# A delta-rule attention with a gated feed-forward network: a first pair prepared apart, 48-row transfers, matmuls on zeros and a new order

## The chip, the cores and the metric

The kernel runs on one core of a Trainium2 chip. The metric is the device time of one execution in microseconds (us), less being better. Engines are called as in the profile: PE (TensorE matmul), PEld (its weight load), DVE (VectorE), ACT (ScalarE), POOL (GpSimd) and SP (SyncE, which here only issues transfers). "SPq" and "ACTq" are the issues of transfers on SP and ACT.

## The reference

Four batches of eight heads run a recurrence over 768 steps with a 40 x 40 state each; its outputs go through a small gated network.

```python
for t in range(S):                      # S = 768, D = 40, B = 4, H = 8
    y[:, :, t] = einsum('bhd,bhde->bhe', rt, state)
    Sa = einsum('bhde,bhe->bhd', state, at)
    state = state * wt[:, :, None, :] - einsum('bhd,bhe->bhde', Sa, bt) \
            + einsum('bhd,bhe->bhde', vt, kt)
x = y.transpose(0, 2, 1, 3).reshape(B, S, 320)
h = maximum(x @ w_in, 0)                # w_in is 320 x 1024
conv = sum over k of conv_w[k] * h shifted by k - 1   # 3 taps along S
out = (h * sigmoid(conv)) @ w_out       # w_out is 1024 x 320
```

## The kernel before

The 768 time steps are cut into 24 chunks of 32, called steps n here, and two steps make a pair j (12 pairs). The network works on windows of two steps (12 windows). A pair is prepared with no knowledge of the state; only the "chain" carries the state from one step to the next.

Preparing a pair: `load_wakb` brings w, a, k and b into three rotating tiles in0 to in2. `decays` turns w on PE (tile pw) and makes running products by scans on DVE (suf, pre). `decayed` turns a (pa), writes ah, spreads ah by six transfers into a64, then turns k and b (pk, pb), writes kt and spreads it by six transfers into k64. `spread` cuts each half into three transfers of 40 rows. `scores` multiplies a64 and k64 on PE (ps), and DVE masks the result into "at". `solve_in` sends "at" to DRAM (bd) and back in another layout (bb). `solve` inverts 128 triangular 32 x 32 matrices at once: 31 rounds of a product (st) and a sum (xx), on DVE for five pairs and on POOL for seven, by the letters of SOLVER ("vgggvgvgvgvg"). It ends with xx going to DRAM (xd) and back (tt), all on SP. `hats` turns kt into kb for the chain.

A step of the chain: pp from the state and v, psb on ACT, pu from tt and psb on PE, vu copies on DVE and ACT, pn on PE, the new state on DVE, and its decay (L665) on POOL. `vturn`, `sturn`, `pairs`, `from_state` and `outputs` make the chunk's outputs, `finish` scales them into xh and xl, and `moe_pack` moves some rows of xh and xl by two transfers. `moe_in` and `moe_out` are the network's matmuls (ph and po) with their work on ACT and DVE. The weights arrive as 64-bit floats in 23 pieces (wi, cv, wo, wp). DVE converts each in seven instructions (L278 to L295), and for wi ACT and POOL make the high and the low part (wih, L311, and wil, L313).

Each piece of work is a generator that yields between its parts. ORDER is a list of some 2,000 tokens ("so0*3" is three parts of solve 0), which `emit_all` goes through; so the order within each engine is written out by hand, and an engine works its queue in order. SP issues nearly all transfers in the order of these tokens; for pair 0 alone `queue` sends half of the loads and of the spreading transfers by ACT. POOL and DVE share the two buffers of the tag stmp for st.

Of the kernel before, what the change touches and what calls it, by code (L numbers as in the profile page):

```python
# [8 lines left out]
F32 = mybir.dt.float32  # L9
# [9 lines left out]
C = 32  # L19
# [4 lines left out]
    ld=3, kb=3, pre=3, kt=1, ah64=2, at=3, bb=2, xx=2, stmp=2,  # L24
    tt=2, psb=1, sd=1, vu64=1, ms=1, xf=1, xh=2, xl=2, hb=2, cc=2, o=1,
# [3 lines left out]
    dd="decayed", sc="scores", ha="hats", si="solve_in", so="solve", co="combine",  # L29
    ch="chain", rt="rturn", vt="vturn", st="sturn", pa="pairs",  # L30
    fs="from_state", ou="outputs", fi="finish", pk="pack", mi="moe_in", mo="moe_out", en="end",
# [8 lines left out]
lr1*2 we16 ch1*2 ha3 dd2 vt0 ou0*2 fi0 we18 we14 fi0 ch1 ha3 dd2*2 ch1 so1*2 dd2*2 vt1*2 so1 we18  # L40
so1*2 fs1*2 ld3*2 rt1 ch1 ch2 we17 we0 we15*2 dd2 so1 pa1 rt1 ch2 we20 pa1 ou1 de3 we17 fi0 we21 fi0
ou1 fi1*2 st2*2 fi1*2 pk0 de3 we19 ch2*3 sc4*2 lv3 sc5*2 si2 ha4*2 ch2*3 ro0 fs2 vt2*2 we21 mi0.0*4
ch3 st3*2 we19 ch3*2 dd3*3 mi0.1 we22 si2 ch3*2 mi0.0 fs2 pa2*2 we20 mi0.1*2 mi0.0 vt3*2 ou2*2 ha5
so2 ch3 ha5 ch3 mi0.0 mi0.3 fi2*2 lr2 mi0.2 lr0 fi2 mi0.0 so2*2 ld3*2 dd3 mi0.3*3 dd3 mi0.1*2 dd3
# [977 lines left out]
```

## Time and profile before

| | before |
|---|---|
| median of 3 runs | 639.4 us (637.51 to 640.18) |
| profiled execution | 637.57 us, its span 635.8 us |
| PE | 533.7 us busy (84%) |
| DVE | 450.4 us (71%) |
| ACT, POOL | 268.1 us, 264.3 us (42% each) |
| mean granted clock of PE | 0.911 of full speed |
| DMA | 66.84 MB, 105 GB/s on average |

The page cuts the span into 40 slices and gives the busy tenths of each engine in them. PE's digits begin with 2624267 and are at 7 to 9 from then on, so the first 100 us differ from the rest. DVE begins with 4898899. The chain that ended last is 29% PE, 17% POOL, 16% DVE, 16% DMA and 8% SP's issues. Durations stand in one profiled execution, whose time lies 1.8 us under the median of the runs.

### The profile page before, as it was taken

To read this page: it belongs to the slowest core of one execution; us is meant where nothing else is said; L and a number is where in the kernel's file an instruction comes from. 1 tells how busy PE (TensorE), PEld (TensorE's weight loads), DVE (VectorE), ACT (ScalarE), POOL (GpSimd) and SP (SyncE) were. 2 spreads that over 40 slices of the span, in tenths; PEclk is the share of its full clock that TensorE was granted. 3 is DMA by queue.
4 is the path that set the end of the run, shared out by engine and by line. 5 is a ranking of instruction groups with operands and counts; after the bars stand their busy time and mean duration, and the time that the engine had idled before them with its cause. 6 is when DMAs were issued, how large, how long until landed. Compare 5 with 4: busy or idle time off the path is not lost.

```text
span 635.8 us, 28901 instructions
## 1 busy us (share of the span) xinstructions
PE 533.7 (84%) x12729; PEld 450.9 (71%) x12729; DVE 450.4 (71%) x1030; ACT 268.1 (42%) x568; POOL 264.3 (42%) x532
## 2 busy tenths in 40 slices
PE   2624267798989878899899799899999899999998
PEld 1523256687877767778778698687888678887884
DVE  4898899978775488577687476788677776472661
ACT  4010122445543424445424456324646226563662
POOL 5110368228888201288301585102684104881100
PEclk9555657999999979899999989799999999999999
DMA  8969748568665377476586654564754754211101
GB/s 144 163 116 147 137 93 182 134 113 134 119 115 117 72 122 134 95 123 118 106 138 109 121 114 86 111 119 85 129 113 73 135 109 90 40 30 46 25 10 38
DMA packets 266517, 66.84 MB, mean 105 GB/s; under 512 B 239536, under 2 KB 260936, under 8 KB 266392
## 3 DMA queue, kind: packets, MB, share of 16 engines
q1 hardware_dynamic: 260052, 63.62, 54.8%
q10 hardware_dynamic: 6340, 1.38, 1.2%
q8 instruction: 100, 1.64, 1.1%
q14 instruction: 25, 0.20, 0.1%
HBM read 38.30 MB, written 10.22 MB: 76 GB/s over the span
## 4 chain that ended last, share of the span: by engine, by line
PE 29%; POOL 17%; DVE 16%; DMA 16%; issue 10%; SPq 8%; ACT 4%; POOLq 0%; DVEq 0%; ACTq 0%
POOL xx L580 7%; POOL st L574 7%; PE ph L819 7%; PE po L866 5%; DMA bb<-bd 3%; DMA bd<-at 3%; DMA xd<-xx 3%; DVE cc L848 3%; PE ps L518 2%; DVE xx L580 2%; POOL state L665 2%; DVE st L574 2%; PE pm L720 2%; DMA in<-in_w_dram 2%; SPq L553 2%
## 5 line engine op out<-in xcount | busy, mean ns | idle before, releaser
L848 DVE SCALAR_TENSOR_TENSOR cc<-hb,cw,cc 128x256 f32<-128x256 f32 x192 | 96.5, 562 | 36.2 <-ACT cc L840 36.1
L866 PE MATMUL po<-wo,g 128*128 128x320 f32 x384 | 116.7, 441 | 0.4 <-DVE g L858 0.4
L574 POOL TENSOR_TENSOR st<-xx,bb 128x126 f32<-128x126 f32 (+22 forms) x217 | 88.7, 409 | 39.0 <-DMA bb<-bd 13.9
L580 POOL TENSOR_TENSOR xx<-xx,st 128x126 f32<-128x126 f32 (+22 forms) x217 | 92.0, 424 | 17.0
L665 POOL TENSOR_TENSOR state<-state,a 104x640 f32<-104x640 f32 x23 | 36.6, 1592 | 136.8 <-DVE state L660 108.4
L866 PEld LDWEIGHTS po<-wo,g 128*128 128x128 f32 x384 | 68.3, 190 | 23.2 <-DVE g L858 0.9
L819 PE MATMUL ph<-xh,wih 120*128 120x256 f32 x288 | 72.7, 312 | 0.8 <-issue 0.8
L796 POOL TENSOR_TENSOR xl<-xf,xh 120x384 fp32r<-120x384 f32 x24 | 24.5, 1020 | 95.0 <-ACT xh L794 95.0
L518 PE MATMUL ps<-a,k 104*64 104x64 f32 x768 | 33.1, 246 | 24.0 <-DMA k<-kt 19.6
L819 PEld LDWEIGHTS ph<-xh,wih 120*128 120x128 f32 x288 | 49.0, 194 | 3.7 <-ACT hb L833 0.8
L858 DVE TENSOR_TENSOR g<-cc,hb 128x512 f32<-128x512 f32 x48 | 34.9, 731 | 21.6 <-ACT cc L853 21.3
L574 DVE TENSOR_TENSOR st<-xx,bb 128x56 f32<-128x56 f32 (+22 forms) x155 | 42.3, 273 | 10.4 <-DMA bb<-bd 5.5
L518 PEld LDWEIGHTS ps<-a,k 104*64 104x64 f32 x768 | 29.6, 158 | 28.0 <-issue 21.1
L580 DVE TENSOR_TENSOR xx<-xx,st 128x56 f32<-128x56 f32 (+22 forms) x155 | 41.2, 266 | 5.3
L853 ACT ACTIVATE cc<-cc 128x512 f32<-128x512 f32 x48 | 30.2, 630 | 33.5 <-DVE cc L848 33.4
L694 ACT COPY v<-pv 128x1024 f32<-128x1024 f32 x24 | 24.3, 1013 | 46.4 <-PE pv L674 46.3
L840 ACT ACTIVATE cc<-hb,cw 128x256 f32<-128x256 f32 x96 | 43.5, 501 | 0.1
L833 ACT ACTIVATE hb<-ph 128x512 f32<-128x512 f32 x48 | 28.5, 595 | 33.5 <-PE ph L819 33.5
L636 DVE COPY vu<-pu 32x320 f32<-32x320 f32 x48 | 23.7, 493 | 26.1 <-PE pu L624 25.0
L819 PE MATMUL ph<-xl,wih 120*128 120x256 f32 x192 | 39.3, 287 | 0.0
L819 PE MATMUL ph<-xh,wil 120*128 120x256 f32 x192 | 39.2, 286 | 0.0
L684 ACT COPY r<-pr 64x1024 f32<-64x1024 f32 x24 | 24.1, 1005 | 21.2 <-PE pr L674 16.2
(287 smaller groups left out, 1076.0 us busy)
## 6 DMA issues: line engine op xcount, KB each, us to landing
bb<-bd SPq DMA_DIRECT2D x24, 256.0 KB
k<-kt SPq DMA_DIRECT2D x46, 120.0 KB
a<-ah SPq DMA_DIRECT2D x33, 121.9 KB
rin<-in_r_dram SPq DMA_DIRECT2D x24, 160.0 KB
vu<-in_v_dram SPq DMA_DIRECT2D x96, 40.0 KB
in<-in_w_dram SPq DMA_DIRECT2D x23, 160.0 KB
in<-in_a_dram SPq DMA_DIRECT2D x23, 160.0 KB
in<-in_k_dram SPq DMA_DIRECT2D x23, 160.0 KB
```

What stands on the lines that cost most here:

```text
L518: nc.tensor.matmul(ps[half(z), h * 64 : h * 64 + 64], k64[:SR, NH * c + h, z], pd["a64"][:SR, NH * (2 * z + c) + h, 1:], start=True, stop= ...
L574: eng.tensor_tensor(t3, xx[:, 0:nj, i : i + 1].to_broadcast([128, nj, nt]), bb[:, i : i + 1, i + 1 :].to_broadcast([128, nj, nt]), ALU.mult,)
L580: eng.tensor_tensor(xx[:, 0:nj, i + 1 :], xx[:, 0:nj, i + 1 :], t3, ALU.add)
L665: nc.gpsimd.tensor_tensor(new, new, al.to_broadcast([SR, 2, H, D]), ALU.mult)
L796: nc.gpsimd.tensor_tensor(wd["xl"][:, :, :, tw], xf, xh.bitcast(F32), ALU.subtract)
L819: nc.tensor.matmul(ph[:, j], l[:, fs], x, start=(j == 0 and i == 0), stop=(i == len(passes) - 1), skip_group_check=True,)
L833: nc.scalar.activation(out=hb[:, :, :, 2 : W + 2], in_=ph, func=AF.Relu)
L840: nc.scalar.activation(out=cc[:, j], in_=hb[:, j, :, 1 : W + 1], func=AF.Copy, scale=cw[:, 1, f : f + 1],)
L848: nc.vector.scalar_tensor_tensor(out=cc[:, j], in0=hb[:, j, :, x : W + x], scalar=cw[:, x, f : f + 1], in1=cc[:, j], op0=ALU.mult, op1=ALU ...
L853: nc.scalar.activation(out=cc, in_=cc, func=AF.Sigmoid)
L858: nc.vector.tensor_tensor(g, cc, hb[:, :, :, 1 : W + 1], ALU.mult)
L866: nc.tensor.matmul(po[:rows, :DM], parts(f), wo[:, f, :], start=(f == 0), stop=(f == NF - 1))
```

## The change

- The new function `keys` holds what was the second half of `decayed`: turning k and b, writing kt and spreading it into k64. It has tokens of its own ("ke"). kt becomes one fixed tile with 128 rows.
- For pair 0 the loads come in the order w, k, a, b. For pair 0 the bd, bb and tt transfers alternate between SP and ACT, as the loads did.
- `spread` takes the number of rows: 48 instead of 40 for a64 (both halves) and for the second half of k64; the first half of k64 stays at 40. The extra rows of the sources are cleared once. In `moe_pack` the transfer within xh carries 48 rows, that from xh to xl stays at 40.
- In `decayed` the small copies on ACT (L478, now L481) come before the products on DVE. `decays` has a further yield.
- The clears of a64 and r64 on ACT become a generator ("cl") and stand behind the copies into ah of pair 0.
- `stmp` becomes one buffer for DVE's solves and one, `stg`, for POOL's.
- `warm`: six blocks of four matmuls of a zero matrix with xini, 512 columns each, written to a bank that nobody reads. One stands ahead of the scores (ps) of pair 0, the others ahead of first matmuls ph of windows 0, 3 and 7 and ahead of the transposes of pair 4 (pw) and pair 5 (pk).
- ORDER is drawn anew as a whole.

```diff
-        for x, nm in ((w, "w"), (a, "a"), (k, "k"), (b, "b")):
-            t = ins[(4 * pd["j"] + "wakb".index(nm)) % len(ins)]
+        for i, nm in enumerate("wkab" if pd["j"] == 0 else "wakb"):
+            x = dict(w=w, a=a, k=k, b=b)[nm]
+            t = ins[(4 * pd["j"] + i) % len(ins)]
...
-    def spread(pd, eng, dst, src):
+    def spread(pd, ns, dst, src):
         for y in range(2):
+            n = ns[y]
             for i in range(3):
-                to = dst(half(y, D), y)[:, i::3]
-                queue(pd, y, eng).dma_start(to, src(slice(i * D, i * D + D), y)[:, : to.shape[1]])
+                to = dst(half(y, n), y)[:, i::3]
+                queue(pd, y).dma_start(to, src(slice(i * D, i * D + n), y)[:, : to.shape[1]])
...
         spread(
-            pd, nc.sync, lambda rows, y: k64[rows].rearrange("p n z t -> p n (z t)"),
+            pd, (D, 48), lambda rows, y: k64[rows].rearrange("p n z t -> p n (z t)"),
...
-            nc.sync.dma_start(
+            queue(pd, bi % 2).dma_start(
                 bd[nb * bi : nb * bi + nb].rearrange("n s t -> s n t"),
...
-            nc.sync.dma_start(bb[q * NBL : (q + 1) * NBL], bd)
+            queue(pd, q).dma_start(bb[q * NBL : (q + 1) * NBL], bd)
...
-            tmp = buf(wn, [128, 144], "stmp", f"st{j}_{i}")
+            tmp = buf(wn, [128, 144], "stmp" if SOLVER[j] == "v" else "stg", f"st{j}_{i}")
...
-        nc.sync.dma_start(xh[2 * D : GR, 2].bitcast(F32), xh[0:D, 2].bitcast(F32))
+        nc.sync.dma_start(xh[2 * D : 128, 2].bitcast(F32), xh[0:48, 2].bitcast(F32))
...
+    def warm(i):
+        pz = bank(f"warm{i}")
+        for _ in range(4):
+            nc.tensor.matmul(
+                pz[:, 0:512], zst, xini.rearrange("p j t -> p (j t)"), start=True, stop=True, skip_group_check=True,
+            )
+        yield
...
-we4 we0 ld0*2 de0*2 ld0*2 we3 we2 dd0 ld1 dd0*8 ha1 we0 de1*2 we0 we2*2 we0 we2 we6 we3 we2 sc0 we4
+fs0 we1 ld0*2 de0 ld0*2 we0 we1*3 we2 dd0 de0 dd0 de0 cl0*2 ke0 we4 dd0 ke0*3 dd0 ke0 ha0*2 we4*2
```

What the new ORDER does is seen in the instructions of an engine. In the rows below a number behind a name is the buffer's; wi10q is the piece of w_in that is being converted, xx_437 and xx_440 are the matrices of solve 0, xx_749 and xx_783 those of solve 1.

DVE at the start of solve 0, before: the last instruction of a conversion, kt of pair 1 from b, and the solve.

```order
L295 TENSOR_TENSOR wi10q<-wi10q 120x256
L495 TENSOR_TENSOR kt_375<-pb_399,suf 120x6x64
L495 TENSOR_TENSOR kt_375<-pb_399,suf 120x6x2x32
L567 CAST xx_437<-xini 128x512
L574 TENSOR_TENSOR st_0_439<-xx_437,bb_361 128x31
```

DVE now, at the end of solve 0, where kt of pair 1 stands:

```order
L591 TENSOR_TENSOR xx_440<-xx_440,st_30_555 128x16
L506 TENSOR_TENSOR kt<-pk_485,suf 120x6x2x32
L506 TENSOR_TENSOR kt<-pk_485,suf 120x6x64
L506 TENSOR_TENSOR kt<-pb_567,suf 120x6x64
L506 TENSOR_TENSOR kt<-pb_567,suf 120x6x2x32
L284 TENSOR_SCALAR wi02q<-wi02r 120x256
```

kt of pair 1 has moved from ahead of solve 0 to behind it.

DVE in the middle of solve 0, before:

```order
L574 TENSOR_TENSOR st_11_472<-xx_437,bb_361 128x120
L580 TENSOR_TENSOR xx_437<-xx_437,st_11_472 128x6x20
L278 TENSOR_SCALAR wi22q<-wi22r 80x256
L282 TENSOR_SCALAR wi22q<-wi22r 80x256
L286 SCALAR_TENSOR_TENSOR wi22q<-wi22r,wi22q 80x256
L290 SCALAR_TENSOR_TENSOR wi22q<-wi22q 80x256
L291 TENSOR_SCALAR wi22q<-wi22q 80x256
L292 SCALAR_TENSOR_TENSOR wi22q<-wi22r,wi22q 80x256
L295 TENSOR_TENSOR wi22q<-wi22q 80x256
L574 TENSOR_TENSOR st_12_515<-xx_437,bb_361 128x133
L580 TENSOR_TENSOR xx_437<-xx_437,st_12_515 128x7x19
```

DVE in the middle of solve 0 now:

```order
L585 TENSOR_TENSOR st_10_478<-xx_440,bb_334 128x126
L591 TENSOR_TENSOR xx_440<-xx_440,st_10_478 128x6x21
L585 TENSOR_TENSOR st_11_481<-xx_440,bb_334 128x120
L591 TENSOR_TENSOR xx_440<-xx_440,st_11_481 128x6x20
L585 TENSOR_TENSOR st_12_494<-xx_440,bb_334 128x133
L591 TENSOR_TENSOR xx_440<-xx_440,st_12_494 128x7x19
```

The conversion of wi22 between the rounds 11 and 12 has left the solve (as have that of wi21 and the two masks of pair 1 between the rounds 19 and 20), so that its rounds follow one another from the first to the last.

POOL in the middle of solve 1, before, with four subtractions for wil and the decay of step 0's new state in it:

```order
L580 TENSOR_TENSOR xx_749<-xx_749,st_11_784 128x6x20
L313 TENSOR_TENSOR wil<-wi12q,wih 120x256
L313 TENSOR_TENSOR wil<-wi23q,wih 80x256
L665 TENSOR_TENSOR state_140<-state_140,a_119 104x16x40
L313 TENSOR_TENSOR wil<-wi13q,wih 120x256
L313 TENSOR_TENSOR wil<-wi03q,wih 120x256
L574 TENSOR_TENSOR st_12_1145<-xx_749,bb_558 128x133
```

POOL now, ahead of solve 1:

```order
L319 TENSOR_TENSOR wil<-wi22q,wih 80x256
L676 TENSOR_TENSOR state_140<-state_140,a_119 104x16x40
L319 TENSOR_TENSOR wil<-wi02q,wih 120x256
L578 CAST xx_783<-xini 128x512
L585 TENSOR_TENSOR st_0_785<-xx_783,bb_748 128x31
L591 TENSOR_TENSOR xx_783<-xx_783,st_0_785 128x31
```

The decay of the state stands ahead of solve 1; two subtractions (wi12, wi23) are left within it, behind its eighth round, and the other two stand behind it.

## Rows read from the trace of the kernel before

**Rows 1.** Stages: us, busy PE, PEld, DVE, ACT, POOL; clock, DMA share, GB/s

```profile
0.00:123.00 123.00, 59.79 (x1129) 50.71 (x1129) 103.71 (x258) 27.67 (x46) 48.30 (x107) 0.65 0.76 137
123.00:180.00 57.00, 53.32 (x1211) 47.36 (x1212) 45.84 (x88) 27.76 (x57) 36.18 (x84) 0.97 0.74 129
180.00:375.00 195.00, 173.18 (x4739) 147.02 (x4738) 131.72 (x304) 83.43 (x179) 86.61 (x172) 0.96 0.62 113
375.00:630.00 255.00, 244.46 (x5645) 205.03 (x5645) 169.17 (x383) 128.51 (x287) 93.16 (x172) 0.99 0.42 80
```

**Rows 2.** Waits of PE after 128 us, the k64 transfers: us, times, longest

```profile
PE ps L518 <- DMA k<-kt: 0.5, 2, 0.3
```

**Rows 3.** Timeline, start: start us, us, engine, line, operation, [idle before]

```profile
8.99 0.87 PE L442 MATMUL pw<-ident,in 128*120 128x128 f32 x3 [7.00 <-DMA in<-in_w_dram]
...
18.10 1.02 DVE L495 TENSOR_TENSOR kt<-pb,suf 120x384 f32<-120x384 f32 x2 [1.30 <-PE pb L442]
...
33.84 1.28 DVE L524 TENSOR_TENSOR at<-ps,tris 128x512 f32<-128x512 f32 x2
```

**Rows 4.** Timeline, solve 0 to step 0

```profile
43.69 0.59 DVE L574 TENSOR_TENSOR st<-xx,bb 128x31 f32<-128x31 f32 x1
...
50.69 0.28 DVE L278 TENSOR_SCALAR wi22q<-wi22r 80x256 int32<-80x256 int32 x1
...
53.24 0.28 DVE L574 TENSOR_TENSOR st<-xx,bb 128x133 f32<-128x133 f32 x1
...
73.65 0.40 SPq L583 DMA_DIRECT2D xd<-xx  x1
...
80.09 2.45 PE L624 MATMUL pu<-psb,tt 32*32 32x40 f32 x64 [0.80 <-DMA tt<-xd]
```

**Rows 5.** Timeline, solve 1 to step 4

```profile
74.85 0.24 POOL L574 TENSOR_TENSOR st<-xx,bb 128x31 f32<-128x31 f32 x1 [8.97 <-DVE pre L460]
...
85.76 0.77 POOL L313 TENSOR_TENSOR wil<-wi12q,wih 120x256 fp32r<-120x256 f32 x1
...
94.00 0.42 POOL L574 TENSOR_TENSOR st<-xx,bb 128x133 f32<-128x133 f32 x1
...
112.16 0.39 POOL L580 TENSOR_TENSOR xx<-xx,st 128x16 f32<-128x16 f32 x1
...
115.78 0.46 SPq L583 DMA_DIRECT2D xd<-xx  x1
...
123.72 0.99 PE L624 MATMUL pu<-psb,tt 32*32 32x40 f32 x60 [0.55 <-DMA tt<-xd]
...
139.89 0.24 POOL L574 TENSOR_TENSOR st<-xx,bb 128x31 f32<-128x31 f32 x1 [6.62 <-DMA bb<-bd]
...
182.59 1.08 PE L624 MATMUL pu<-psb,tt 32*32 32x40 f32 x60 [0.26 <-DMA tt<-xd]
```

**Rows 6.** Issues by line on SP: duration ns min/median/max, first and last start

```profile
L426 SPq DMA_DIRECT2D k<-kt x69: 767/768/1615, 18.8 to 518.6; - x69
...
L586 SPq DMA_DIRECT2D tt<-xd x48: 325/413/1463, 77.9 to 573.8; - x48
```

**Rows 7.** Groups up to 128 us: count, busy us, mean ns, idle before

```profile
L574 DVE TENSOR_TENSOR st<-xx,bb 128x126 f32<-128x126 f32 (+22 forms) x31 | 8.7, 281 | 1.0
L580 DVE TENSOR_TENSOR xx<-xx,st 128x126 f32<-128x126 f32 (+22 forms) x31 | 8.6, 277 | 1.1
L460 DVE TENSOR_TENSOR_SCAN pre<-pw,dp 120x396 f32<-120x396 f32 x8 | 7.4, 969 | 0.1
```

**Rows 8.** Timeline, the k64 transfers of pair 1 and its scores

```profile
46.28 5.00 SPq L426 DMA_DIRECT2D k<-kt  x6
...
54.90 0.48 PE L518 MATMUL ps<-a,k 104*64 104x64 f32 x4 [14.66 <-DMA k<-kt]
```

**Rows 9.** Timeline, scores of pair 2 on PE

```profile
124.65 3.49 PE L518 MATMUL ps<-a,k 104*64 104x64 f32 x64
```

**Rows 10.** Chain that ended last: start us, us, what

```profile
378.69 0.95 PE ph L819 x8
```

More of the change, by code (lines that the diff above doesn't have):

```diff
@@ L28 @@
     we="weights", ro="rows", ld="wakb", lv="v", lr="r", de="decays",
-    dd="decayed", sc="scores", ha="hats", si="solve_in", so="solve", co="combine",
+    dd="decayed", ke="keys", sc="scores", ha="hats", si="solve_in", so="solve", co="combine",
     ch="chain", rt="rturn", vt="vturn", st="sturn", pa="pairs",
-    fs="from_state", ou="outputs", fi="finish", pk="pack", mi="moe_in", mo="moe_out", en="end",
+    fs="from_state", ou="outputs", fi="finish", pk="pack", mi="moe_in", mo="moe_out", en="end", wa="warm", cl="clears",
@@ L40 @@
[L40 to L44, printed above, removed]
@@ L241, in tile_decay_delta_attention_then_conv_gate_moe @@
         t = cp.tile([128, 4 * NH, 2 * C + 1], F32, name=f"a64{i}")
-        clear(t.rearrange("p n w -> p (n w)"))
         a64s.append(t)
     ah = [
-        cp.tile([GR, NR, (y + 1) * C + 1], F32, name=f"ah{y}") for y in range(2)
+        cp.tile([128, NR, (y + 1) * C + 1], F32, name=f"ah{y}") for y in range(2)
     ]
     nc.gpsimd.memset(ah[1], 0.0)
+    nc.gpsimd.memset(ah[0][96:128], 0.0)
+    kt = cp.tile([128, 2, 2 * G, 4, C], F32, name="kt")
+    nc.gpsimd.memset(kt[96:128, 1], 0.0)
     k64 = cp.tile([128, 2 * NH - 1, 2, 64], F32, name="k64")
@@ L471, in decayed @@
         for y in range(2):
-            nc.vector.tensor_tensor(
-                ah[y][:, :, C * y + 1 : C * y + C + 1], pa[:, y].rearrange("p (n w) -> p n w", w=C),
-                pd["pre"][:, y, :, 0:C], ALU.mult,
-            )
-        yield
-        for y in range(2):
             nc.scalar.copy(
-                ah[y][:, :, 0], suf[:, y * NY : y * NY + NY].rearrange(
+                ah[y][:GR, :, 0], suf[:, y * NY : y * NY + NY].rearrange(
                     "p (n w) -> p n w", w=C + 1
@@ L483, in decayed, with keys @@
         yield
+        for y in range(2):
+            nc.vector.tensor_tensor(
+                ah[y][:GR, :, C * y + 1 : C * y + C + 1], pa[:, y].rearrange("p (n w) -> p n w", w=C),
+                pd["pre"][:, y, :, 0:C], ALU.mult,
+            )
+        yield
         a64 = pd["a64"] = a64s[j % len(a64s)]
         spread(
-            pd, nc.sync, lambda rows, y: a64[rows, :, 0 : C * y + C + 1], lambda rows, y: ah[y][rows],
+            pd, (48, 48), lambda rows, y: a64[rows, :, 0 : C * y + C + 1], lambda rows, y: ah[y][rows],
         )
         yield
-        kt = pd["kt"] = buf(wn, [GR, 2, 2 * G, 4, C], "kt", f"kt{j}")
+    def keys(pd):
+        j = pd["j"]
         for x, nm in enumerate("kb"):
@@ L585, in solve @@
         for bi in range(B):
-            nc.sync.dma_start(
+            queue(pd, bi % 2).dma_start(
                 tt[quad(bi)].rearrange("p c h t -> p (c h t)"),
@@ L913, in tile_decay_delta_attention_then_conv_gate_moe, with clears @@
     BUFS.update(e1=1, e2=1)
+    def clears():
+        for t in a64s:
+            clear(t.rearrange("p n w -> p (n w)"))
+        yield
+        clear(r64.rearrange("p y i z c x t -> p (y i z c x t)"))
+        yield
+    def warm(i):
[3 more added lines that the diff above has]
+                pz[:, 0:512], zst, xini.rearrange("p j t -> p (j t)"), start=True, stop=True, skip_group_check=True,
+            )
+        yield
     pds = [dict(j=j) for j in range(NSTEP // 2)]
@@ L990, in tile_decay_delta_attention_then_conv_gate_moe @@
     put(("end", 0), moe_end)
+    put(("clears", 0), clears)
+    for i in range(NWARM):
+        put(("warm", i), lambda i=i: warm(i))
     with tc.manual_schedule():
```

180 lines of the change are left out of this document (95 added, 85 removed).

## The prediction

> **What bounds the kernel now.** I read the busy time of the engines by stages first [rows 1]. In the first 123 us PE is busy for 59.8 us, at a mean granted clock of 0.65; from there to 630 us it is busy for 471.0 of 507 us, at 0.96 to 0.99. So there are two regimes: a start in which PE waits for data, and a long stretch in which PE's own work sets the pace, with 3.7, 21.8 and 10.5 us of idle time in its three parts. With two clock levels, 2.4 and 1.2 GHz, means of 0.97, 0.96 and 0.99 make (0.03 x 57 + 0.04 x 195 + 0.01 x 255) / 0.5 = 24 us at the lower one. In the second regime PE waits 0.5 us in all for the k64 transfers [rows 2], so what only makes these transfers quicker is worth nearly nothing there.
>
> Then I followed the start in order of time. The first transposes wait for w's load until 8.99 us, kt of pair 0 is finished at 19.12, and the masked scores "at", for which two rows of DVE are enough, only at 35.12, as DVE converts weights first [rows 3]. Solve 0 starts on DVE at 43.69, is interrupted at 50.69 for a conversion, and its result is sent at 73.65; "pu" of step 0 can begin at 80.09 [rows 4]. Solve 1 runs on POOL from 74.85 to 112.55. Its result is sent at 115.78, and step 2 gets its "tt" at 123.72; solve 2 starts at 139.89, and step 4 has its "tt" at 182.59 [rows 5]. This chain of solves paces the start, and DVE, busy 103.7 of 123 us [rows 1], lies under it.
>
> **First loads and pair 0.** One weight transfer of 240 KB stands ahead of w on SP where two did. At the 137 GB/s of the stage [rows 1] it takes 1.8 us; I take 1.2 of that for kt (0 to 1.8): finished at 17.9. The clears move from ACT's idle beginning behind the copies into ah; only a640 is needed at once, and its transfers wait for the product ah1 anyway. Price nothing; if uncovered, the first two clears' few us on ACT. Between kt and "at" DVE now has three conversions. One is the stretch from 50.69 to 53.24, 2.6 us [rows 4], so DVE is free at 25.7, and PE's scores, moved up with kt, end at about 28.3: "at" is done at 29 instead of 35.1. From "at" to the solve it was 8.6 us [rows 3, 4]; bd and bb now go out on SP and ACT, three issues fewer in a row at 0.41 us (that of tt) [rows 6], plus some queueing, so 7 us: bb is there at 36. On DVE a decays step (four scans of 0.97 us [rows 7] and 0.3), a conversion, two ah products and the cast stand ahead, 8.4 us, so solve 0 starts at about 38. Uninterrupted it has 62 instructions of 17.3 us [rows 7] and gaps: end at 56.5, 14 us earlier than now. xd follows at once; from xd to "pu" it was 6.4 us [rows 4], with tt on two queues 6: step 0 at 62.5 instead of 80.1.
>
> **Why these 17 us don't arrive.** kt of pair 1 now stands behind the whole of solve 0 on DVE; it stood ahead. So kt comes at 58.5, and its six transfers stand behind tt on SP, which waits for xd until 61. Six of 40 rows take 5.0 us to issue, and the first landed 3.6 us after the last was issued, the rest a little later [rows 8]; with three of 48 rows I take 3.7 and 4, so 69.5. Scores at the low clock, up to 3.9 us (3.5 in [rows 9]), "at" at 74, bd and bb on SP alone 8.6: solve 1 starts at about 82.6, not at 74.85. It gets shorter. Now 8.2 us of pause for four subtractions and a state lie in it, from 85.76 to 94.00 [rows 5], then two subtractions (1.6): 31 us, end at 113.6 against 112.55. What saves it is the queue: xd waited 3.2 us on SP behind six k64 transfers and now stands behind two loads of r. Sent at 113.7, with the 7.9 us from 115.78 to 123.72 [rows 5], step 2 gets its tt at 121.6: **2 us** earlier. Bounds: 9 earlier (transfers landing at once, scores at the full clock) to 5 later (below).
>
> **Pair 2.** Its scores stood behind "pu" of step 2 on PE (124.65, 3.5 us [rows 9]); now they stand ahead, in what was idle: **3.5 us**. So bd and bb of pair 2 go out right behind tt, and solve 2 can start once step 2's state has left POOL, at about 130: 10 us earlier. Step 4 follows at about 173, not 182.6.
>
> **48 rows.** Nine of a pair's twelve spreading transfers and one of two in the pack step carry 48 rows. An issue of 40 rows takes 768 ns whatever its bytes, one of 32 rows (tt) 413 [rows 6]; 48 rows lie between these or at the upper, so SP gains 0 to 3.2 us a pair. Beyond the start I book nothing [rows 2]; cover gone, it is SP's to lose.
>
> The Trainium skill, page "DMA: Bandwidth & Descriptors", section "Why a DMA increments its semaphore by 16 and not by 1", says that a transfer runs on the largest number of engines, at most 16, that divides the slowest dimension: 10 engines for 40 rows, 16 for 48. By it each engine carries 3 rows instead of 4; an estimate from that is a quarter off the moving part of the 3.6 us that a transfer took to land, so under 0.9 us for each pair, and the sum would gain that once, ahead of solve 1. The 768 against 413 ns agree with a special case for 40 rows; no row shows the engines themselves.
>
> **Zeros.** Each block is four matmuls over 512 columns. The nearest row is eight of 256 columns in 0.95 us [rows 10], so 0.95 a block at the full clock, twice that at the low one. The first block lies in idle time; five more cost 0 (all in idle) to 4.8 us. I take 2.4.
>
> **POOL and DVE temporaries** now have a buffer each; within one engine the products and sums follow one another anyway, so I book 0.
>
> **The redrawn order.** With PE saturated a lead of 10 us in the chain is worth only the idle time that it fills. 21.8 us of it lie in 180 to 375 us, where the chain and PE's queue meet. I take a third, **7.3 us** (0 to two thirds): PE's queue is in order, and other waits come up next.
>
> **Sum.** -2 - 3.5 - 7.3 + 2.4 = -10.4. The profiled execution took 637.57 us around its span of 635.8, and the median of the runs is 639.4, 1.8 above it. So 627.2 for such an execution and **629.0** as the median.
>
> **Rivals.**
> 1. The lead never reaches PE: steps 0 and 1 are early, steps 2 and 3 are not, and idle time in the long stretch stays. -2 - 3.5 + 4.8 = -0.7, so 638.7. For it: PE was busy 53.3 of 57 us already from 123 on [rows 1]. Against it: the start still has 63 us of idle PE. This is also the case in which the change does not do what it says.
> 2. The lead fills two thirds of the idle time (14.5 us), and the clock stays up for half of its 24 low us, of which PE's share of work would take half the time (5.3 us): -2 - 3.5 - 14.5 - 5.3 + 2.4 = -22.9, so 616.5. For it: the stretch with the most idle time, 180 to 375, is also the one with the lowest clock [rows 1]. Against it: an order that is drawn anew has waits of its own. The Trainium skill, page "TensorE: Matmul & The Clock Gate", section "Part 4: PE-mode transpose", says that transposes do not open the clock as matmuls do; by that rule a few matmuls on zeros among transposes would keep it open, with this rival's gain. The rows bear it out in part: 0.65 in the first stage, whose work on PE is largely transposes, but they cannot separate these from the gaps.
> 3. Slower: solve 1 becomes the bound. The mechanism is that kt of pair 1 behind solve 0 delays solve 1 by more than its fewer pauses give back. SP's queue has two weight transfers, each waiting for buffers from POOL or DVE, right ahead of bd of pair 1. The point is a start of solve 1 at 84.7 (its 31 us then end at xd's present 115.78); at 90 step 2 is 5.3 us late, and with all zeros on PE's path 5.3 - 3.5 + 4.8 = +6.6: 646.0. For it: my start of 82.6 has 2 us to spare. Against it: PE can do the network's matmuls in such a wait.
>
> **How the numbers follow.** The forecast, from 620 to 635, 0.52; rival 1 (636 to 642) 0.20; rival 2 (608 to 620) 0.16; rival 3 (643 to 655) 0.12. The range 613 to 642 leaves out the lower half of rival 2 and nearly all of rival 3. A measurement of this kernel tells about 0.5% (3.2 us) from no change: faster 0.68, same 0.20, slower 0.12.
>
> **What would show it.** In the profile after: "at" of pair 0 near 29 us and "pu" of step 0 near 62; solve 1's first row on POOL near 82.6 and its last near 113; "pu" of step 2 near 121, solve 2's start near 130, "pu" of step 4 near 173; PE idle from 180 to 375 us about 7 us smaller. If solve 1 starts late, or step 4 comes early and PE's idle time stays, the forecast is wrong at that step.

## The result: slower by 1%

| | before | after |
|---|---|---|
| median of 20 runs each | 637.5 us | 643.2 us |
| range of the runs | 631.9 to 643.1 | 638.5 to 646.5 |
| span of the profiled execution | 635.8 us | 643.4 us |
| PE busy | 533.7 us | 544.1 us |
| PE idle (span less busy) | 102.1 us | 99.3 us |

The ratio is 1.010, 95% interval 1.007 to 1.013. Ratios here and below leave out, on both sides, the runs that lie over 1.5% above the fastest of their kernel, and medians keep them, so the two differ by up to 1% (1.4% in e8, where two of six runs are left). In the profiled execution (645.07 us) PE's idle time has shrunk by 2.8 us, and PE's busy time has grown by 10.4.

The stages of [rows 1] for the kernel after (columns as there):

```profile
0.00:123.00 123.00, 66.51 (x1129) 56.12 (x1129) 101.11 (x250) 25.84 (x43) 49.06 (x109) 0.67 0.84 143
123.00:180.00 57.00, 48.42 (x1156) 42.64 (x1156) 37.91 (x80) 23.04 (x44) 36.42 (x86) 0.82 0.69 125
180.00:375.00 195.00, 176.56 (x4712) 148.60 (x4714) 135.70 (x315) 87.80 (x188) 79.26 (x151) 0.98 0.62 112
375.00:630.00 255.00, 243.42 (x5744) 206.16 (x5737) 173.68 (x388) 130.91 (x291) 98.51 (x190) 0.99 0.48 87
```

A stage's length less the first busy time is PE's idle time: 56.5, 8.6, 18.4 and 11.6 us, against 63.2, 3.7, 21.8 and 10.5 before. The start gave 6.7 us and the middle 3.4; the stretch from 123 to 180 us took 4.9 back, the last stage 1.0 and what lies behind 630 us 1.3. The stretch from 123 to 180 us is also where the granted clock fell, from a mean of 0.97 to 0.82; a transpose pa took 351 ns there in the mean, for 277 before.

The steps that the prediction named, from the timeline of the kernel after, by time (the timelines of DVE, PE, POOL and SP put together):

```profile
28.67 0.69 DVE L535 TENSOR_TENSOR at<-ps,tris 128x512 f32<-128x512 f32 x1 [1.01 <-PE ps L529]
...
38.34 0.19 DVE L585 TENSOR_TENSOR st<-xx,bb 128x31 f32<-128x31 f32 x1
...
63.46 2.07 PE L635 MATMUL pu<-psb,tt 32*32 32x40 f32 x64 [3.06 <-DMA tt<-xd]
...
82.59 0.31 POOL L585 TENSOR_TENSOR st<-xx,bb 128x31 f32<-128x31 f32 x1 [4.40 <-DMA bb<-bd]
...
112.42 2.16 SPq L402 DMA_DIRECT2D in<-in_k_dram  x2
...
113.09 0.23 POOL L591 TENSOR_TENSOR xx<-xx,st 128x16 f32<-128x16 f32 x1
...
113.38 1.91 PE L685 MATMUL pr<-ident,rin 128*128 128x128 f32 x8
...
115.32 2.12 SPq L412 DMA_DIRECT2D rin<-in_r_dram  x2
117.54 0.64 SPq L594 DMA_DIRECT2D xd<-xx  x1
...
120.26 1.29 PE L612 MATMUL pp<-state,a 40*32 40x40 f32 x64 [2.42 <-POOL state L676]
...
126.53 1.43 PE L547 MATMUL pz<-ident,kt 120*128 120x120 f32 x6 [2.18 <-DVE pre L469]
127.89 1.29 PE L635 MATMUL pu<-psb,tt 32*32 32x40 f32 x64
...
135.04 0.24 POOL L585 TENSOR_TENSOR st<-xx,bb 128x31 f32<-128x31 f32 x1
...
164.65 2.27 POOL L676 TENSOR_TENSOR state<-state,a 104x640 f32<-104x640 f32 x1 [5.35 <-DVE state L671]
...
173.16 0.23 POOL L591 TENSOR_TENSOR xx<-xx,st 128x16 f32<-128x16 f32 x1
...
184.09 0.79 PE L635 MATMUL pu<-psb,tt 32*32 32x40 f32 x64
```

Up to the end of solve 1 the forecast holds to 1 us: "at" at 29.4 (29), solve 0 from 38.3 (38), step 0 at 63.5 (62.5), solve 1 from 82.6 (82.6) to 113.3 (113.6). Then xd waits 4.2 us on SP: 1.3 us behind two loads of k, 0.7 until "pr" on PE has read the tile of r, and 2.1 for the issues of the two loads of r. Step 2 comes at 127.9, later than before (122.7 to 123.7) and not earlier. No wait for tt stands ahead of its pu: PE waits 2.42 us for the state on POOL ahead of the first pp, and 2.18 us for a scan on DVE ahead of pz. Solve 2 starts 4.9 us sooner than before, but in it POOL stands 5.35 us until DVE has the state of step 3, since the decay of that state stands among its rounds; it ends at 173.4, and step 4 begins at 184.1 (182.6 in [rows 5]).

The zeros, by source line (ns min/median/max) and two of their six blocks:

```profile
L937 PE MATMUL warm<-xini,zst x24: 378/379/634, 19.1 to 487.4; 128*128 128x512 bf16 x24
```

```profile
19.07 1.76 PE L937 MATMUL warm<-xini,zst 128*128 128x512 bf16 x4
139.54 1.04 PE L937 MATMUL warm<-xini,zst 128*128 128x512 bf16 x4
```

One block at 1.76 us and five at 1.03 to 1.04 make 6.9 of PE's 10.4 us more. The other 3.5 are the same matmuls taking longer: those of the scores (ps) alone are busy for 37.6 us, 33.1 before. Single executions don't settle such a split: the changed kernel without zeros shows 538.7 to 543.0 us of busy PE (e4, e11, g2), and the kernel before with the zeros alone 533.9 (f2).

### The profile page after: what moved, and what is told of

Read it like the earlier page. It is cut to its first block, busy times and chain, and to the rows that moved or that the text cites. A ratio compares the mean times of both kernels' runs of the same rounds, so it can differ in the third digit from the quotient of the medians.

```text
span 643.4 us, 28952 instructions
## 1 busy us (share of the span) xinstructions
PE 544.1 (85%) x12753; PEld 458.7 (71%) x12753; DVE 448.8 (70%) x1030; ACT 268.9 (42%) x568; POOL 263.3 (41%) x534
## 4 chain that ended last, share of the span: by engine, by line
PE 57%; DMA 12%; DVE 12%; SPq 8%; issue 6%; ACT 3%; POOL 1%; ACTq 0%; DVEq 0%; POOLq 0%
PE po L877 12%; PE ph L830 11%; PE ps L529 5%; SPq L434 4%; DMA k<-kt 3%; PE pm L731 3%; PE pn L660 3%; PE py L768 2%; PE pp L622 2%; PE pv L685 2%; PE pp L612 2%; PE pu L635 2%; PE py L754 2%; PE pz L547 2%; PE pt L715 2%
## 5 line engine op out<-in xcount | busy, mean ns | idle before, releaser
L859 DVE SCALAR_TENSOR_TENSOR cc<-hb,cw,cc 128x256 f32<-128x256 f32 x192 | 91.4, 538 | 33.2 <-ACT cc L851 33.1
L591 POOL TENSOR_TENSOR xx<-xx,st 128x126 f32<-128x126 f32 (+22 forms) x217 | 89.0, 410 | 17.0
L529 PE MATMUL ps<-a,k 104*64 104x64 f32 x768 | 37.6, 260 | 15.9 <-DMA k<-kt 7.7
L529 PEld LDWEIGHTS ps<-a,k 104*64 104x64 f32 x768 | 32.9, 170 | 21.2 <-issue 12.2
L591 DVE TENSOR_TENSOR xx<-xx,st 128x56 f32<-128x56 f32 (+22 forms) x155 | 43.9, 284 | 5.3
L647 DVE COPY vu<-pu 32x320 f32<-32x320 f32 x48 | 23.7, 493 | 29.4 <-PE pu L635 28.4
L660 PEld LDWEIGHTS pn<-vu,kb 64*64 64x64 f32 (+1 forms) x1472 | 26.8, 135 | 9.5 <-ACT vu L649 4.1
```

Of the source, the lines that this page charges most:

```text
L529: nc.tensor.matmul(ps[half(z), h * 64 : h * 64 + 64], k64[:SR, NH * c + h, z], pd["a64"][:SR, NH * (2 * z + c) + h, 1:], start=True, stop= ...
L591: eng.tensor_tensor(xx[:, 0:nj, i + 1 :], xx[:, 0:nj, i + 1 :], t3, ALU.add)
L660: nc.tensor.matmul(pn[half(y, m), z, h * D : h * D + D], kf[half(z), y * HD + h * D : y * HD + h * D + m], vu[half(z), y, h, 0:D], start=T ...
L859: nc.vector.scalar_tensor_tensor(out=cc[:, j], in0=hb[:, j, :, x : W + x], scalar=cw[:, x, f : f + 1], in1=cc[:, j], op0=ALU.mult, op1=ALU ...
```

## The experiments

Each line has its own median and that of the kernel before measured beside it. e1 to e4, e5 to e8, e9 to e12, f1 to f4 and g1 with g2 were measured together and share the kernel before. Its times scatter by 4.1 us (standard deviation of 147 runs), so a median of 6 or 12 runs leaves 2 us and more open.

| run | median | before | ratio (95%) |
|---|---|---|---|
| e1 order before | 649.3 | 639.0 | 1.0202 (1.0134 to 1.0271) |
| e2 new start | 648.8 | 639.0 | 1.0138 (1.0066 to 1.0210) |
| e3 old start | 647.8 | 639.0 | 1.0172 (1.0107 to 1.0237) |
| e4 no zeros | 638.1 | 639.0 | 1.0009 (0.9968 to 1.0051) |
| e5 old order, clean | 643.3 | 640.4 | 1.0027 (0.9984 to 1.0070) |
| e6 old start, clean | 639.5 | 640.4 | 1.0020 (0.9971 to 1.0068) |
| e7 r and pz behind | 639.6 | 640.4 | 1.0070 (1.0029 to 1.0111) |
| e8 40 rows, no zeros | 640.8 | 640.4 | 0.9871 (0.9782 to 0.9961), 6 runs from 629 to 642 |
| e9 path cleared | 642.5 | 639.7 | 1.0101 (1.0058 to 1.0144) |
| e10 old to step 4 | 641.1 | 639.7 | 1.0071 (1.0019 to 1.0123) |
| e11 no zeros | 641.0 | 639.7 | 1.0054 (1.0008 to 1.0101) |
| e12 40 rows, no zeros | 636.1 | 639.7 | 0.9965 (0.9910 to 1.0019) |
| f1 before with 48 rows | 643.2 | 639.3 | 1.0075 (1.0034 to 1.0116) |
| f2 before with zeros | 638.2 | 639.3 | 1.0011 (0.9966 to 1.0056) |
| f3 after with 40 rows | 639.9 | 639.3 | 1.0036 (1.0000 to 1.0072) |
| f4 40 rows, no zeros | 639.2 | 639.3 | 1.0019 (0.9976 to 1.0061) |
| g1 after | 646.3 | 640.8 | 1.0151 (1.0083 to 1.0219) |
| g2 no zeros | 643.0 | 640.8 | 1.0127 (1.0055 to 1.0199) |

### Code or order, start or rest

e1 carries the changed code in the order of the kernel before (the ORDER of the kernel after is replaced):

```diff
-fs0 we1 ld0*2 de0 ld0*2 we0 we1*3 we2 dd0 de0 dd0 de0 cl0*2 ke0 we4 dd0 ke0*3 dd0 ke0 ha0*2 we4*2
+cl0*2 we4 we0 ld0*2 de0*3 ld0*2 we3 we2 dd0 ld1 dd0*3 ke0*5 ha1 we0 de1*3 we0 we2*2 we0 we2 we6 we3
...
-NWARM = 6
+NWARM = 0
```

> The changed code (48-row transfers, the loads of pair 0 in the order w, k, a, b and on two queues, a buffer each for POOL's and DVE's products, k and b apart from a) with the instructions in the order of the kernel before, and without the matmuls on zeros. Theory O (the new order makes the loss, the code nothing): 637.5 us as the kernel before, within 0.5%. Theory C (the code's transfers make it, for instance by their 3% more bytes): 641 to 645 us. If the code gains what its shorter issues suggest (some 0.125 us less for each of 9 transfers a pair): 634 to 637 us, with the gain at the start alone.

649.3 us, 2% slower, which neither theory had. Two traps of its own explain part of it. With the loads in the order w, k, a, b the old order loads w of pair 1 into the tile of k ahead of its use (so this run and e3 compute pair 0 with w of pair 1 in place of k, with the same work), and two transfers of tt wait on ACT's queue behind a cast that waits for DVE:

```profile
18.04 1.51 PE L445 MATMUL pk<-ident,in 128*120 128x128 f32 x6 [4.69 <-DMA in<-in_w_dram]
```

```profile
82.90 0.26 PE L630 MATMUL pu<-psb,tt 32*32 32x40 f32 x2 [0.75 <-ACT psb L623]
87.23 0.34 PE L630 MATMUL pu<-psb,tt 32*32 32x40 f32 x4 [4.08 <-DMA tt<-xd]
```

So the change of queue and of load order does harm under an order that was not drawn for it. e2 and e3 cut both orders at the first matmul of window 0:

```diff
-vt2*2 fs2 dd3*3 fs2 pa2*2 fi1 we7 ro0 pk0 de0 mi0.1 ou2 wa1 ou2 we18 mi0.1 we18 we9 mi0.0*2 lv3
+we18 we20 we19 lv3 ch2 mi0.0*4 ch3 st3*2 we19 ch3*2 mi0.1 we22 si2 ch3*2 mi0.0 we20 mi0.1*2 mi0.0
```

(e2, the seam; e3 is the reverse, the old start of e1's diff and then the new order.)

> The changed code with the new order up to the first matmul of window 0, then the kernel before's order for all that is left (one block of zeros, ahead of the scores of pair 0). Theory S (the loss arises at the start, where pu of step 2 came at 127.9 us and not at 122.7, with the clock low until 136.6): 642 to 646 us, pu of step 2 at 127 to 128. Theory R (it arises in the order of the rest): 635 to 639 us.

> The reverse: the kernel before's order up to the first matmul of window 0, then the new order for all that is left, with five blocks of zeros. Theory S: 635 to 640 us (the five blocks are 5.2 us of PE, some of them in idle time). Theory R: 642 to 646 us. If both this and the run with the new start are at 640 to 642, the loss is shared between the two parts.

Both lie above every range, 648.8 and 647.8, so the two theories are not told apart: a seam moves what one order had done and the other not to one place, and e3 has e1's traps. e5 and e6 take the traps out (loads and queues of pair 0 as before):

```diff
-        for i, nm in enumerate("wkab" if pd["j"] == 0 else "wakb"):
+        for i, nm in enumerate("wakb"):
...
-            queue(pd, bi % 2).dma_start(
+            nc.sync.dma_start(
```

> As the run with the order before, but the loads of pair 0 in the old order and bd, bb and tt on SP alone, since in that run w of pair 1 was loaded into the tile of k of pair 0 ahead of its use and two of four tt transfers stood on ACT behind a wait for DVE until 85 us (pu of step 0 waited 4.1 us for them). What is left of the change is 48-row transfers, a buffer each for POOL's and DVE's products and the later place of k and b in the code. Theory O (the code by itself does nothing): 637 to 641 us, within 0.5% of the kernel before. Theory C (the extra bytes cost): over 643 us. If shorter issues gain: 633 to 636 us.

> The kernel before's order up to the first matmul of window 0 (loads and queues of pair 0 as before), then the new order for all that is left, without zeros. Theory S (the new start costs some 10 us of PE's work by 180 us, and the new order of the rest gains as much): 627 to 632 us. Rival (what the rest gains is only the start's loss given back, since PE's work waits for its place): 636 to 641 us.

e5 came at 643.3 by the median, theory C's time; its ratio is not clear of 1, but the mean of all its runs is 4.0 us above that of the kernel before beside it (two standard errors are 2.3). That turned the suspicion to the 48 rows. e6 is at 639.5: the rival's number, no gain in the rest by itself. In its trace step 2 is on time at 122.2 us, but step 3 comes at 149.4, where before it came at 138.3: the stretch from 123 to 180 us is thin in the new order itself, whatever its start (PE is idle for 9.7 us in it, 3.7 before). e10 keeps the old order up to step 4 and so leaves that stretch out (the seam, against e5's order):

```diff
-mi1.3 dd4*2 mi1.3*3 mo1.0 ch4*2 mo0.1 ch4*2 ou1 mi1.1*2 vt1 vt4 lv6 vt4 fs4*2 mi1.1 pa4*2 mi1.1*2
+mi1.3 dd4*2 mi1.3*3 mo1.0 ch4 ld0 we4 si1 we21 de0 dd1 ke2 mi0.1 so0 we13 ke0 ha5 we8 ch4*3 vt4 lv6
```

> The kernel before's order up to pu of step 4 (182 us), then the new order, without zeros, loads and queues of pair 0 as before. From 180 to 430 us PE's idle time is 25.0 us in the kernel before and 18.8 to 20.8 with the new order. Theory M (the new order of the middle is better by itself): PE idle from 123 to 180 us 4 us and from 180 to 430 us 19 to 21 us, 632 to 636 us. Rival D (the middle only works off what its own start left): 25 us idle from 180 to 430, 639 to 643 us.

From 180 to 430 us, after and e10:

```profile
180.00:430.00 250.00, 229.16 (x5917) 193.30 (x5916) 179.41 (x413) 113.36 (x243) 101.90 (x196) 0.98 0.64 114
```

```profile
180.00:430.00 250.00, 227.47 (x5991) 192.89 (x5990) 179.90 (x421) 110.15 (x235) 106.72 (x207) 0.97 0.67 117
```

PE is idle for 20.8 us in the kernel after and 22.5 in e10, against 25.0 before. The same stretch differs between executions of one kernel: 18.8, 20.6 and 22.0 in e4, e11 and g2, which are one kernel in the new order, and 23.0 to 26.7 in f2, f1 and e5 in the old one. So the new order's middle does close some idle time, and whether a part of that is work left over from the thin stretch is not shown by e10. The time, 641.1, is rival D's, and the gain that theory M forecast did not come.

### Single waits

e7 takes two waits ahead of step 2 away, e9 three more (both without zeros):

```diff
-ch1 ch2 we10 lr2 de3 fi1*2 st2*2 ch2*2 ha4*2 so1 sc4 si2 we9 de3 ch2*2 we9 ch2*2 we10 vt2*2 fs2
+ch1 ch2 we10 de3 fi1*2 st2*2 ch2*2 so1 sc4 si2 lr2 we9 de3 ch2*2 ha4*2 we9 ch2*2 we10 vt2*2 fs2
```

> The changed kernel without zeros, and two moves: the loads of r of pair 2 go out on SP behind xd, tt, bd and bb instead of ahead of xd of solve 1 (which waited 4.2 us for them), and pz of step 4 stands behind pu of step 2 on PE instead of ahead of it (it waited 2.2 us for a scan on DVE). Theory Q (these two waits delay step 2, and the chain from there on): pu of step 2 at 122 to 124 instead of 126 to 128, 633 to 636 us. Rival L (the lead doesn't reach PE's end): pu of step 2 as early, but 637 to 640 us.

```diff
-we21 ke2 we10*2 ou1*2 dd2 sc5 so1 fi1 lr1 rt1*2 so1*3 fi0*2 sc4 de3 we9 fi0 we12*3 ch1 ld3 sc5 ld3
-ch1 ch2 we10 de3 fi1*2 st2*2 ch2*2 so1 sc4 si2 lr2 we9 de3 ch2*2 ha4*2 we9 ch2*2 we10 vt2*2 fs2
+we21 ke2 we10*2 ou1*2 dd2 sc5 so1 fi1 lr1 rt1*2 so1*3 fi0*2 sc4 de3 we9 we12*3 ch1 ld3 sc5 ld3 ch1
+fi0 ch2 we10 de3 fi1*2 st2 ch2*2 st2 so1 sc4 si2 lr2 we9 de3 ch2*2 ha4*2 we9 ch2*2 we10 vt2*2 fs2
...
-vt3*2 fs3 ld4 ke2 ld4 we20 lv4 mi0.1 mi0.0 fi2 mi0.1 fs3 pa3 sc7 pa3 fi2 sc6*2 sc7 ou3*2 si3 ch3
+vt3*2 fs3 ld4 ke2 ld4 we20 lv4 mi0.1 mi0.0 fi2 mi0.1 fs3 pa3*2 fi2 ou3*2 ch3 mi0.1 so2 ch3 mi0.1
+mi0.0 mi0.1 sc7 sc6*2 sc7 si3 so2*2 mi0.2 fi3 mi0.0 mi0.1 fi2 ch3 de4 mi0.3*2 ch4*2 so0 fi3*2 mi0.2
```

> The run with r and pz behind, and three more moves: xl of step 0 behind the state's decay on POOL (the decay waited 2.7 us for it), the copy sd behind psb of step 2 on ACT, and the scores of pair 3 behind three more parts of window 0 on PE (which stood 1.9 to 2.7 us idle ahead of them). Theory W (single waits of the new order between 110 and 165 us are what costs there): pu of step 2 at 123, PE's idle time from 123 to 180 us down from 8 to 10 to about 5 us, 634 to 636 us. Rival V (other waits take their place): idle time from 123 to 180 us as before the moves, 638 to 641 us.

pu of step 2 in e7, then in e9, and e9's stretch:

```profile
125.52 0.87 PE L635 MATMUL pu<-psb,tt 32*32 32x40 f32 x64 [0.63 <-ACT psb L628]
```

```profile
122.80 0.23 PE L635 MATMUL pu<-psb,tt 32*32 32x40 f32 x2 [1.30 <-ACT sd L722]
```

```profile
123.00:180.00 57.00, 46.17 (x1068) 40.63 (x1068) 38.25 (x81) 21.63 (x42) 36.47 (x87) 0.80 0.72 128
```

In e7 xd is sent at 115.1 instead of 117.5, but step 2 did not come at 122 to 124, because xl stood ahead of the state's decay on POOL, and pp and psb behind it. In the kernel after it is the same pair of rows:

```profile
117.97 0.99 POOL L807 TENSOR_TENSOR xl<-xf,xh 120x384 fp32r<-120x384 f32 x1 [4.65 <-ACT xh L805]
118.92 1.29 POOL L676 TENSOR_TENSOR state<-state,a 104x640 f32<-104x640 f32 x1
```

With that moved too, e9 has step 2 at 122.8, 5 us earlier than the kernel after. PE's idle time from 123 to 180 us is then 10.8 us, not 5, and the time is no better (642.5; e11, the same kernel without these moves, measured together with it, 641.0). Theories Q and W fall. Of rival L the time came (639.6) and not the early step 2; of rival V the idle time came, and a time above its 638 to 641. The chain's lead at step 2 is not what the time follows.

### Zeros

```diff
-NWARM = 6
+NWARM = 0
```

(and the tokens wa0 to wa5 left out), three times: e4, e11 and g2, the last measured together with the kernel after (g1).

> The changed kernel without its six blocks of matmuls on zeros (1.76 us and five of 1.03 to 1.04 us in its trace). If they lie on PE's path and do nothing for the clock: 5.2 us less, 638 us. If they lie in idle time: 643 us. If they hold the clock up, its low time of 117.6 us grows and the time is over 643 us.

> The changed kernel without zeros once more, beside the next run: 637 to 640 us.

> The changed kernel as it is, beside the next run: 642 to 645 us.

> The changed kernel without its six blocks of zeros, in the same call. If the zeros lie on PE's path here: 3 to 5 us less than the run beside it. If they cost nothing, as in the kernel before: within 1 us of it.

f2 puts them alone into the kernel before:

```diff
+    def warm(i):
+        pz = bank(f"warm{i}")
+        for _ in range(4):
+            nc.tensor.matmul(
+                pz[:, 0:512], zst, xini.rearrange("p j t -> p (j t)"), start=True, stop=True, skip_group_check=True,
+            )
+        yield
```

> The kernel before with the six blocks of zeros alone, each where the changed kernel has it (ahead of the scores of pair 0, of first matmuls of windows 0, 3 and 7, of the transposes of pairs 4 and 5). If five blocks lie on PE's path: 5.2 us more than the kernel before, 643 to 645 us. If half of them fall into idle time, as forecast: 641 to 642. If they hold up the clock: fewer us at the lower clock than 111.6 and no more time than before.

In the new order they cost 5.1 (e4) and 2.2 us (e11) against the 643.2 of the kernel after, which was measured apart from them, 3.3 us where both were measured together (g1, g2), and 0.7 with 40 rows (f3, f4). In the kernel before they cost nothing that can be told (638.2 against 639.3). So a cost of 1 to 5 us in the new order is likely, its size is not settled, and why the old order doesn't show it stays open. e11 (641.0) and g1 (646.3) lie 1 us above what was expected of them.

No run shows that the zeros hold the clock. The profiled execution of f2 has a granted clock of 0.933 where the kernel before has 0.911, but over all runs measured together the mean is 0.924 with zeros and 0.930 without; in the new order it is 0.914 with them (after) and 0.918 and 0.916 without (e4, e11), 0.918 with and 0.915 without where both were measured together (g1, g2).

### 48 rows

e8, e12 and f4 are one kernel, the changed one with 40 rows and without zeros; f3 keeps the zeros:

```diff
-            pd, (48, 48), lambda rows, y: a64[rows, :, 0 : C * y + C + 1], lambda rows, y: ah[y][rows],
+            pd, (D, D), lambda rows, y: a64[rows, :, 0 : C * y + C + 1], lambda rows, y: ah[y][rows],
...
-            pd, (D, 48), lambda rows, y: k64[rows].rearrange("p n z t -> p n (z t)"),
+            pd, (D, D), lambda rows, y: k64[rows].rearrange("p n z t -> p n (z t)"),
```

> The changed kernel without zeros, with all spreading and packing transfers at 40 rows again. If the 48 rows gain only SP's time, off the path: 638 us as with 48 rows, within 0.5%. If they are worth more in this order (7.7 us of issues of k64 and a64 less in ten pairs, landings up to a quarter sooner, ahead of scores that wait for them 7.7 us in all): 641 to 645 us. If the 3% more bytes hurt: 633 to 636 us.

> The same with all spreading and packing transfers at 40 rows, once more: if 48 rows are worth nothing here, within 0.5% of the run beside it; the first such run had a median of 640.8 us with a spread from 629 to 642.

> The changed kernel with all its spreading and packing transfers at 40 rows, zeros kept. Theory T: 639 to 641 us against 643.2. Rival: 643.

> The changed kernel with 40 rows and without zeros, a third time: 636 to 638 us, 2 to 4 us under the kernel before. If it is within 1 us of the kernel before, the new order gains nothing by itself.

(In e8, e12, f3 and f4 the transfer within xh goes back to 40 rows too; the cut above leaves that out.) f1 is the kernel before with that diff the other way round, and k64's source in a tile of 128 rows; its transfer within xh stays at 40 rows:

> The kernel before with one thing changed: the spreading transfers into a64 (both halves) and into the second half of k64 carry 48 rows, nine of twelve a pair. Theory T (the longer transfers slow the others on the DMA engines, so that PE waits for loads, tt and k64): 642 to 645 us, the first queue's share 59 to 60% instead of 54.8%, PE's waits for DMA after 123 us 8 to 12 us instead of 3.5. Rival (the rows cost nothing, the run with the old order lost its 4 us elsewhere): 637 to 640 us.

f1 is 643.2 against 639.3 us, ratio 1.0075 and clear of 1: theory T's time. The clears of the extra rows at its start do not explain that, as pu of step 0 begins at 79.5 us there and at 80.1 before. In the new order e11 and e12, measured together, stand 5.0 us apart, and f3 is 3.3 us under the kernel after, which was measured apart from it; e4 and e8, also measured apart, show no such difference. f4, at 639.2, missed the 636 to 638 that was expected. The first DMA queue's packets, MB and share of the 16 engines' span, for the kernel before, f1 and f4:

```profile
q1 hardware_dynamic: 260052, 63.62, 54.8%
```

```profile
q1 hardware_dynamic: 268784, 65.66, 59.5%
```

```profile
q1 hardware_dynamic: 258820, 63.09, 52.7%
```

3.4% more packets take 4.7 points more of the engines' time. The share times the span times 16 engines, over the packets, is 21.4 ns for a packet before and 22.8 in f1, at the same mean size (245 and 244 bytes): the mean packet takes 6% longer. All kept traces say the same: 20.7 to 21.5 ns in the six executions with 40 rows, 22.0 to 22.9 in the fourteen with 48. In the issues the opposite is seen, here f1's:

```profile
L430 SPq DMA_DIRECT2D a<-ah x69: 582/659/1877, 15.3 to 519.4; - x69
```

659 ns in the median, where a 40-row issue took 768 [rows 6]. Who waits for the packets differs between executions: PE's waits for DMA after 123 us are, in the kernel before and in e5 (old order, 48 rows):

```profile
PE pb L442 <- DMA in<-in_b_dram: 1.7, 1, 1.7
PE pu L624 <- DMA tt<-xd: 1.3, 4, 0.5
PE ps L518 <- DMA k<-kt: 0.5, 2, 0.3
```

```profile
PE pb L445 <- DMA in<-in_b_dram: 4.0, 2, 2.5
PE ps L524 <- DMA k<-kt: 3.3, 5, 1.2
PE pu L630 <- DMA tt<-xd: 2.4, 8, 0.9
PE pp L617 <- DMA vu<-in_v_dram: 0.9, 1, 0.9
PE ph L825 <- DMA xh<-xh: 0.8, 1, 0.8
```

3.5 us become 11.4, but 5.0 in f1, where theory T forecast 8 to 12, so this path explains e5 and not all of f1. Of the 7.0 us by which f1's span is longer than that of the kernel before, 4.1 are busy time of PE, for the same matmuls (537.8 against 533.7). Whether the extra bytes or another spread over the DMA engines make the packets slow was not told apart.

The versions side by side, each as the mean of all its runs less that of the kernel before measured beside it (two standard errors are 1.7 to 2.6 us):

| version | runs | us more than before |
|---|---|---|
| new order alone (e8, e12, f4) | 30 | -1.1 |
| new order, 48 rows (e4, e11, g2) | 30 | 1.6 |
| new order, zeros (f3) | 12 | 2.1 |
| new order, both: the kernel after (its 20 runs above, g1) | 26 | 5.4 |
| old order, 48 rows (f1) | 12 | 4.4 |
| old order, zeros (f2) | 12 | 0.1 |

So the 48 rows cost 2.7 and 3.3 us in the new order and 4.4 in the old one, the zeros 3.2 and 3.8 in the new order and nothing in the old one. Each of the four differences within the new order has an uncertainty of about 3 us, so their sizes are rough; f1's 4.4 us, with 2.2, is clear of zero.

## Why the prediction was wrong

The forecast was 629.0 us in a range of 613 to 642; the kernel took 643.2, and the sign was wrong: 10.4 us less were forecast and 5.7 more came. The base of the sum, 639.4 from three runs, lay 1.9 us above the median of 20 runs; that is not what failed. By its terms:

- **First loads, pair 0, solve 0, solve 1: right.** Five times within 1 us, and the saying that the 17 us of step 0 would not arrive. This is what reading a chain in order of time can do.
- **Step 2, 2 us earlier: wrong, it was 4.2 later.** The step that failed is "xd [...] now stands behind two loads of r. Sent at 113.7": it gives these loads 0.1 us, as if their issues were over when solve 1 ends. xd was sent at 117.5, behind two loads of k, the wait of r's load for pr, and the issues of r. And the step let pu wait for tt alone: pz behind a scan and the state's decay behind xl came later still. e9, with all of them moved, has step 2 at 122.8 and is no faster, so this miss did not decide the time.
- **Scores of pair 2 in idle time, 3.5 us, and the lead filling a third of the idle time, 7.3 us: gone.** Solve 2 did start earlier (135.0 for 130), but its lead was lost to a wait of 5.35 us on POOL, and PE's idle time fell by 2.8 us in all, where the three terms together are 12.8. The mistake was to price a lead in the chain without pricing the new order's own gaps: e6 has step 2 on time and still step 3 11 us late. The new order alone (e8, e12, f4) is 0.5 us slower, 3.6 faster and 0.1 faster than the kernel before by the medians, 1.1 faster by the means: 0 to 3 us of gain, not 12.8. That is nearest to rival 1, whose mechanism is a lead that never reaches PE. Nor does the sum ask whether the same matmuls take longer in the new order. In the three executions of e8, e12 and f4 PE is idle for 97.9 to 102.1 us and busy for 538.8 to 541.2, for 102.1 and 533.7 before.
- **48 rows, "nothing", bounded only by a gain: wrong, and the cause that is shown best.** 3.9 us by the medians in the kernel before (f1, alone and clear of noise), about 3 in the new order by the means. The step that failed is that more rows for a transfer were costed on SP's issue alone. [rows 2], which show that quicker transfers are worth nothing, were read as if slower ones cost nothing. The stage's DMA share of 0.62 to 0.76 [rows 1] stood in the table, and a transfer with a fifth more bytes on a shared resource had no lower bound below nothing. The Trainium skill, page "DMA: Bandwidth & Descriptors", section "Why a DMA increments its semaphore by 16 and not by 1", spoke for 48 rows by its rule of the number of engines (16 for 48 rows, 10 for 40). No run here shows the engines themselves. The issue did get shorter (659 for 768 ns), but the measured time goes against a gain, and the measurement decides.
- **Zeros, 2.4 us of 0 to 4.8: about within its bounds** (0.7 to 5.1 in the new order by the medians, 3.2 and 3.8 by the means). The price of one block, 0.95 or twice that, was 1.03 and 1.76 us.
- **Rival 2 and the clock.** Nothing of it came: in the two profiled executions the time at the lower clock moved from the start and the middle into 123 to 180 us, where the mean fell from 0.97 to 0.82, and over all runs the mean granted clock is 0.914 for the kernel after (20 runs) and 0.931 for the kernel before (127). The Trainium skill's page "TensorE: Matmul & The Clock Gate", section "Part 4: PE-mode transpose", from which the rival drew, is neither shown nor refuted by the zeros here. That the 0.65 of the first stage comes from its transposes is not borne out: f1 had 0.99 there with the same transposes.
- **Rival 3** had the sign, with a start of solve 1 that came as forecast and not late; step 2 was late, but by another wait, and e7 and e9 show that this is not the price.

Put together from the runs: the order 0 to 3 us of gain, the 48 rows about 3 us of loss (4 in the old order), the zeros 1 to 5 us of loss, for a measured loss of 5.7. Shown are these shares; why the zeros cost in one order only, and by which waits the slower packets reach PE, stays open. No version beats the kernel before clearly: the new order with 40 rows and no zeros is at 636.1, 639.2 and 640.8 us, beside 639.7, 639.3 and 640.4 for the kernel before.

## What to carry to other kernels

When loads are found ahead of something urgent in a queue, add up what stands there at that time: the issues of every load (here 1.3 and 2.1 us), and what each load's tile still waits for (0.7). And follow every input of the step that is to come earlier, not only the one that was late before: with the loads of r and pz moved away, step 2 waited for the state on POOL. Once PE is dense, a lead in the chain is worth only the idle time that the new order really closes, so sum PE's idle time by stages of both orders, and ask of each idle stretch which work stands behind it. Bytes that are added for a better shape go to a resource that all transfers share: bound them on both sides, and try them alone in the old kernel first.

## What was not expected of the hardware

The granted clock of the start does not tell how fast PE worked there. f1's first 123 us and its pu of step 2:

```profile
0.00:123.00 123.00, 60.07 (x1125) 50.53 (x1125) 104.03 (x258) 27.48 (x46) 49.29 (x109) 0.99 0.87 141
```

```profile
123.15 0.25 PE L628 MATMUL pu<-psb,tt 32*32 32x40 f32 x2 [1.69 <-ACT psb L621]
```

The matmuls of the scores up to 90 us, in the kernel before and in f1 (count, busy us, mean ns, idle before), then those of the kernel before from 180 to 375 us:

```profile
L518 PE MATMUL ps<-a,k 104*64 104x64 f32 x128 | 8.4, 318 | 19.5 <-DMA k<-kt 19.0 <-issue 0.3
```

```profile
L522 PE MATMUL ps<-a,k 104*64 104x64 f32 x128 | 8.4, 318 | 20.3 <-DMA k<-kt 20.3
```

```profile
L518 PE MATMUL ps<-a,k 104*64 104x64 f32 x256 | 9.5, 224 | 3.5 <-issue 2.9 <-DVE xf L784 0.4
```

The granted clock was 0.99 in f1's first 123 us and 0.65 in the kernel before [rows 1], with the same order and the same sparse work on PE. PE was busy for 60 us in both, a matmul of the scores took 318 ns in both, a transpose pa 425 and 426 ns, and step 2 came at the same time. From 180 to 375 us the scores take 224 ns. So neither the matmuls nor the chain followed the granted clock in this stretch; what sets the 318 ns is not shown. Nor is that level a property of the kernel: over 127 executions of the kernel before, the mean granted clock lies between 0.899 and 0.981, and the time hardly follows it (correlation -0.13).
